# A convolution with a mixture of experts behind it: the copies of a turn ahead of its rests, and one of the weight rests on GpSimd

## The chip, the core and the metric

The kernel runs on one core of one Trainium2 chip. The metric is the device time of one execution in microseconds. What is timed is the whole launch: loads from the chip's memory, all the work, and the stores of the result.

The engines are named as in the profile: PE (TensorE, matrix multiplication), PEld (its weight loads), DVE (VectorE), ACT (ScalarE), POOL (GpSimd), SP (SyncE, which only issues transfers here). Each works off a queue of its own in order. What an engine in front of a wait has behind it in its queue stands still with it.

## The reference

```python
def _attn_ref(x, weight):                 # x (8, 2880, 192), weight (8, 7)
    w = softmax(weight)                   # over the 7 taps of each of 8 heads
    x_pad = np.concatenate([np.zeros((B, 6, D)), x], axis=1)
    ...
    out = np.einsum('hk,bskhg->bshg', w, x_unf)   # causal, 24 channels a head

def _moe_ref(x, w_group, w_expert, w1, w2):       # x (23040, 192)
    g_logits = x @ w_group                        # 4 groups
    g_idx = np.argmax(g_logits, axis=1)
    ...
    for g in range(4):
        e_logits = xg @ w_expert[g]               # 4 experts in a group
        e_idx = np.argmax(e_logits, axis=1)
        ...
            h = np.maximum(xg[mask_e] @ w1[g, e], 0.0)    # 192 -> 1024
            ye = h @ w2[g, e]                             # 1024 -> 192
            out[tok_idx] = (g_w * e_w)[:, None] * ye
```

Each token is first mixed with the six before it, then sent to the best expert of its best group. Only that one of the 16 experts works on it, and the result is weighted by the product of the two softmax values.

## The kernel before

**Two streams of work on one PE.** The router takes the 23040 tokens in 18 units of up to 12 blocks of 120 tokens. Per unit it does the convolution (L452), copies it out of PSUM (L461), stores the mixed rows to memory, computes the 20 logits (L475 to L507), takes softmax and argmax on DVE (L539 to L568), and works out each token's place in the list of its expert (L579 to L626). A matmul of one-hot rows (L633) builds the list, DVE makes it whole numbers (L640, L642), and POOL scatters it into a table in memory (L645) at rows that L626 works out. A unit is a generator, so its pieces are laid between the pieces of the other stream, and the two share every queue.

The other stream is the experts, in slots of 256 tokens. As soon as 5 units are routed, experts 0 to 9 get one slot each (portion 0 of the program, `pi == 0`, from about 115 to 250 us); after 9 units experts 10 to 12 get two, after 12 units experts 13 to 15 three; what is left of each expert's five comes in the last portion, by pairs of slots (`pair`, from about 465 us), and 18 slots of a tail take the remainder.

**A slot.** POOL gathers 256 rows by the list (L717). `turn` transposes them into one PSUM tile `px` and splits them into a high part, a copy rounded to the matmul's format on ACT (L755, `xh`), and a low part, the rest that the rounding left, on DVE (L756, `xl`). The last 64 of the 192 channels go into `xb`, copy and rest in the upper and lower 64 rows: as one copy L766 and one rest L767, or, where the turn is `packed`, as two copies L762 and two rests L763, by turns. A matmul with five products (L817; L786 in a pair) makes the hidden values, ACT and DVE take relu and its rest (L822 and L823; L790 and L791), and two products (L835, L839; L801, L805) lead back to 192 channels. ACT scales them (L897), DVE adds (L898), and POOL scatters the rows into the result (L888).

**Two readers of one tile.** Where ACT and DVE read the same PSUM tile, the framework lets them do so one after the other, in the order in which the program names them. In `turn` all copies and rests read `px`. So a copy that stands behind a rest waits for that rest to end.

**Weights.** `weights()` loads an expert's matrices over SP's queue (L666 to L671) and returns four steps, which `split_one` lays between the matmuls: the first 128 channels of the first matrix into a copy and a rest (`ah` L682 on ACT, `al` L683 on DVE), its last 64 channels (`bh` L690 on ACT, `bl` L691), and the second matrix in two halves (`cw`, L697 on ACT, L698 on DVE). Which engine makes a rest is set by a map, `eng.get(k, nc.vector)`, with 1 for the last 64 channels. For the experts of the portions the map comes from `PENG`, which was empty; experts 0 and 1 are loaded ahead, with a map of their own (empty, before and after); the tail's 18 slots already have POOL make L691. The raw matrices lie in a ring of three buffers (`raw`), so that a load waits for the last rest of the matrix that lay there.

Of the kernel before, what the change touches and what calls it, by code (L numbers as in the profile page):

```python
# [9 lines left out]
F32 = mybir.dt.float32  # L10
# [5 lines left out]
AF = mybir.ActivationFunctionType  # L16
ALU = mybir.AluOpType
# [3 lines left out]
P = 128  # L21
# [3 lines left out]
SLOT = 256  # L25
# [11 lines left out]
def conv_moe_kernel(  # L37
# [10 lines left out]
    nc = tc.nc  # L48
# [26 lines left out]
    D2 = D - P  # L75
# [36 lines left out]
    NTAIL = NBIG + NSMALL  # L112
    LAG = 3
    REST = 10
    PENG = lambda pi, e: None
    NQK = 5
    QREST = 6
    QGA = 0
# [149 lines left out]
    def clear_table():  # L268
# [12 lines left out]
        out=tri, in_=ones, pattern=[[1, P]], compare_op=ALU.is_gt, fill=0.0, base=0, channel_multiplier=-1,  # L281
# [12 lines left out]
    for nb in sorted({n for _, n in units}):  # L294
# [35 lines left out]
        out=sel, in_=ident.rearrange("p (e l) -> p e l", e=E), axis=AX.X, op=ALU.add)  # L330
    nc.gpsimd.iota(io[:, 0:1], pattern=[[0, 1]], base=0, channel_multiplier=1)
    nc.vector.tensor_scalar(
        out=io[:, 1:2], in0=io[:, 0:1], scalar1=LE - 1, scalar2=None, op0=ALU.bitwise_and)
# [6 lines left out]
    for g in range(NSK):  # L340
        nc.sync.dma_start(
            out=skew[0:R, g * HG:(g + 1) * HG],
            in_=bass.AP(wvd.tensor, wvd.offset + VL - KS - (BT - 1) + g * HG * VL, [[1, R], [VL, HG], [1, VW]]),
# [21 lines left out]
    for h in range(H):  # L365
        nc.scalar.activation(
            out=band[0:R, h], in_=skew[0:R, h, BT - 1::-1], func=AF.Exp, bias=wm[0:R, h:h + 1],
# [22 lines left out]
    for i in range(NXG):  # L390
        t = const.tile([P, XE + XW], F32, name=f"xg{i}")
# [347 lines left out]
    def turn(xs, n=2, packed=False, into=None, single=False):  # L739
        if into is None:  # L740
            px = pm.tile([P, 512], F32, name="pm")
            xa = ff.tile([P, 2, SLOT], F32R, name="xa")
            xb = ff.tile([P, SLOT], F32R, name="xb")
            xh, xl = xa[:, 0], xa[:, 1]
        else:
            px = pm.tile([P, 512], F32, name="pm") if single else ph.tile([P, 2, SLOT], F32, name="ph").rearrange("p a b -> p (a b)")
            xh, xl, xb = into
        w = n * P
        for t in range(n):
            nc.tensor.transpose(px[:, t * P:(t + 1) * P], xs[t][:, 1:1 + P], ident)  # L750
            if not packed:
                nc.tensor.transpose(px[0:D2, SLOT + t * P:SLOT + (t + 1) * P], xs[t][:, 1 + P:XW], ident)
        if packed:
            nc.tensor.transpose(px[:, SLOT:SLOT + P], xs[0][:, 1 + P:XE], ident)
        nc.scalar.activation(out=xh[:, 0:w], in_=px[:, 0:w], func=AF.Copy)  # L755
        nc.vector.tensor_tensor(out=xl[:, 0:w], in0=px[:, 0:w], in1=xh[:, 0:w].bitcast(F32), op=ALU.subtract)  # L756
        if packed:
            for t in range(2):
                hi, lo = slice(t * D2, (t + 1) * D2), slice((1 - t) * D2, (2 - t) * D2)
                cs = slice(t * P, (t + 1) * P)  # L760
                pb = px[hi, SLOT:SLOT + P]
                nc.scalar.activation(out=xb[hi, cs], in_=pb, func=AF.Copy)  # L762
                nc.vector.tensor_tensor(out=xb[lo, cs], in0=pb, in1=xb[hi, cs].bitcast(F32), op=ALU.subtract)  # L763
            return None if into else (xa, xb)
        pb = px[0:D2, SLOT:SLOT + w]
        nc.scalar.activation(out=xb[0:D2, 0:w], in_=pb, func=AF.Copy)  # L766
        nc.vector.tensor_tensor(out=xb[D2:P, 0:w], in0=pb, in1=xb[0:D2, 0:w].bitcast(F32), op=ALU.subtract)  # L767
        return xa, xb

    def pair_room():  # L770
        hi = ff.tile([P, 2, SLOT], F32R, name="xa").rearrange("p a b -> p (a b)")
# [4 lines left out]
    def turn_half(X, k, xs, single=False):  # L776
        cs = slice(k * SLOT, (k + 1) * SLOT)
        turn(xs, 2, True, [x[:, cs] for x in X], single)
# [435 lines left out]
    def open_slot(i):  # L1214
# [20 lines left out]
        else:  # L1235
            W = pre.pop(e if pi == 0 else None, None) or weights(e * D, e * F, PENG(pi, e)) if s == 0 else opened[i - 1][0]
            k = [v for v, _ in portions[pi][1]].index(e)
# [12 lines left out]
    while routed[1] < portions[0][0]:  # L1250
# [5 lines left out]
        for i in [i for i, kk in enumerate(KPRE) if kk == k]:  # L1256
            e, q = divmod(i, 5)
# [13 lines left out]
    if TB:  # L1271
        turned[0] = turn(gathered[0])
# [4 lines left out]
    if not TB:  # L1277
        turned[0] = turn(gathered[0])
# [125 lines left out]
    with tc.If(nrare[0] != 0):  # L1404
# [4 lines left out]
        with tc.For_i(0, nover, 1):  # L1409
            for u in range(NU):  # L1410
# [10 lines left out]
                    out=gi[:, 0], in0=gi[:, 1], scalar1=VS.bit_length() - 1, scalar2=None, op0=ALU.logical_shift_right)  # L1421
# [4 lines left out]
                    out=ee, in0=eoff[0:BT].unsqueeze(1).broadcast_to([BT, nb, E]),  # L1426
                    in1=gb[:, 0].unsqueeze(2).broadcast_to([BT, nb, E]), op=ALU.is_equal,
                )
                nc.vector.tensor_tensor(
                    out=ee, in0=ee, in1=ends[0:BT, u].unsqueeze(1).broadcast_to([BT, nb, E]), op=ALU.mult)  # L1430
# [4 lines left out]
                for k in range(nb):  # L1435
                    nc.gpsimd.indirect_dma_start(
                        out=idtab[:, :], out_offset=bass.IndirectOffsetOnAxis(ap=gi[:, 0, k:k + 1].bitcast(U32), axis=0),
                        in_=idw[:, k:k + 1], in_offset=None,
# [50 lines left out]
```

## Time and profile before

| | before |
|---|---|
| median of 3 runs | 1145.64 us (1144.6 to 1146.14) |
| profiled execution | 1152.26 us |
| span of its instructions | 1150.4 us |
| mean granted clock of PE | 0.977 of full speed |
| PE busy | 1072.8 us, 93% |
| DVE busy | 752.4 us, 65% |
| ACT busy | 644.1 us, 56% |
| POOL busy | 523.5 us, 46% |

The span runs from the first to the last instruction of the profiled execution; launch and end are in its time, not in the span. Busy shares are means over a program whose first 115 us (routing alone), the stretch from 115 to 465 us (routing and experts together), the pairs and the tail differ much. A granted clock of 1.0 is 2.4 GHz, one of 0.5 is 1.2 GHz. A row of the timeline gives the start in us from the span's start, the duration in us, engine, line and operation, what is written and read; at its end, in brackets, how long the engine had been idle and whose end it had waited for.

### The profile page before, as it was taken

What the parts mean: (1) busy time and instruction counts of PE and PEld (TensorE: products, weight loads), DVE (VectorE), ACT (ScalarE), POOL (GpSimd) and SP (SyncE); (2) the same over time, 40 slices, a digit from 0 to 9 for tenths busy, and PEclk for the clock granted to TensorE, in tenths of its full rate; (3) what the DMA queues carried; (4) which work ended last, traced back from release to release, by engine and by line L of the source; (5) the groups of instructions that cost most, each with busy time, mean ns of one, the idle gap of its engine ahead of it and who ended that gap; (6) DMA issues with size and microseconds to landing.
All of it is one profiled execution on the core that took longest, in us unless ns stands there. A gap on an engine that the chain in (4) does not pass through costs nothing.

```text
span 1150.4 us, 20931 instructions
## 1 busy us (share of the span) xinstructions
PE 1072.8 (93%) x7124; PEld 971.1 (84%) x7124; DVE 752.4 (65%) x1671; ACT 644.1 (56%) x1362; POOL 523.5 (46%) x611
## 2 busy tenths in 40 slices
PE   6565999998999998999999999999999999999996
PEld 4444788987989998889899999999999988989986
DVE  3465878987778756576565555655556665687874
ACT  5445657765657554454455445554545555677873
POOL 3004143333334454554545454545445554487773
PEclk9878989999999999999999999999999999999998
DMA  8767688999566432332253223322333435499970
GB/s 185 186 158 228 160 222 215 252 234 216 156 155 164 122 106 85 116 112 67 83 137 113 72 76 99 113 74 73 103 101 106 133 92 157 116 257 257 252 201 19
DMA packets 143167, 166.08 MB, mean 144 GB/s; under 512 B 18946, under 2 KB 124397, under 8 KB 143054
## 3 DMA queue, kind: packets, MB, share of 16 engines
q1 hardware_dynamic: 100974, 111.04, 36.4%
q0 software_dynamic: 18752, 35.85, 10.5%
q10 hardware_dynamic: 23328, 17.80, 6.6%
q8 instruction: 57, 0.93, 0.3%
q14 instruction: 56, 0.46, 0.1%
HBM read 129.43 MB, written 36.58 MB: 144 GB/s over the span
## 4 chain that ended last, share of the span: by engine, by line
PE 70%; DMA 5%; DVE 5%; issue 4%; ACT 3%; POOL 1%; POOLq 0%; ACTq 0%; DVEq 0%
PE ph L786 21%; PE ph L817 11%; PE pm L801 7%; PE po L801 7%; PE po L835 7%; PE pm L805 3%; PE po L805 3%; PE po L839 3%; PE pm L452 3%; DMA rawc<-in_moe_w 2%; DMA xg<-xcd,idpt 2%; DVE hl L823 1%; DVE cw L698 1%; PE ph L852 1%; PE ph L750 1%
## 5 line engine op out<-in xcount | busy, mean ns | idle before, releaser
L888 POOL DMA_INDIRECT out<-ys,idp x160 | 174.3, 1090 | 267.9 <-DVE ys L898 192.0
L791 DVE SCALAR_TENSOR_TENSOR hl<-ph,hh 128x512 fp32r<-128x512 f32 x208 | 142.2, 689 | 141.7 <-ACT hh L790 141.3
L790 ACT ACTIVATE hh<-ph 128x512 fp32r<-128x512 f32 x208 | 123.0, 600 | 170.6 <-PE ph L786 167.6
L717 POOL DMA_INDIRECT xg<-xcd,idp x160 | 175.3, 1096 | 93.8 <-issue 40.5
L835 PE MATMUL po<-cw,hh 128*128 128x384 f32 x592 | 193.2, 379 | 3.0 <-DVE ys L898 3.0
L817 PE MATMUL ph<-xa,ah 128*128 128x256 f32 x592 | 169.2, 307 | 0.0
L839 PE MATMUL po<-cw,hl 128*128 128x192 f32 x592 | 149.6, 253 | 0.0
L801 PE MATMUL po<-cw,hh 128*128 128x384 f32 x416 | 134.1, 359 | 0.0
L801 PE MATMUL pm<-cw,hh 128*128 128x384 f32 x416 | 133.9, 359 | 0.0
L823 DVE SCALAR_TENSOR_TENSOR hl<-ph,hh 128x512 fp32r<-128x512 f32 x148 | 101.1, 684 | 42.7 <-ACT hh L822 42.5
L822 ACT ACTIVATE hh<-ph 128x512 fp32r<-128x512 f32 x148 | 87.9, 596 | 62.3 <-PE ph L817 49.8
L835 PEld LDWEIGHTS po<-cw,hh 128*128 128x128 f32 x592 | 112.7, 190 | 7.6 <-DVE ys L898 3.6
L817 PEld LDWEIGHTS ph<-xa,ah 128*128 128x128 f32 x592 | 113.1, 191 | 4.4 <-issue 1.5
L839 PEld LDWEIGHTS po<-cw,hl 128*128 128x128 f32 x592 | 114.4, 193 | 2.0
L805 PE MATMUL pm<-cw,hl 128*128 128x192 f32 x416 | 104.2, 250 | 0.0
L805 PE MATMUL po<-cw,hl 128*128 128x192 f32 x416 | 104.1, 250 | 0.0
L786 PE MATMUL ph<-xa,ah 128*128 128x512 f32 x208 | 86.0, 413 | 1.4 <-DVE hl L791 1.4
L698 DVE TENSOR_TENSOR cw<-rawc,cw 128x768 fp32r<-128x768 f32 x82 | 76.0, 955 | 15.1 <-ACT cw L697 14.5
L817 PE MATMUL ph<-xb,bh 128*128 128x256 f32 x296 | 84.0, 284 | 0.7 <-DVE xb L767 0.7
L805 PEld LDWEIGHTS po<-cw,hl 128*128 128x128 f32 x416 | 79.1, 190 | 5.8
L817 PE MATMUL ph<-xb,bl 128*128 128x256 f32 x296 | 83.9, 284 | 0.0
L817 PE MATMUL ph<-xa,al 128*128 128x256 f32 x296 | 83.7, 283 | 0.0
(275 smaller groups left out, 2656.2 us busy)
## 6 DMA issues: line engine op xcount, KB each, us to landing
rawc<-in_moe_w SPq DMA_DIRECT2D x82, 384.0 KB
raw<-in_moe_w SPq DMA_DIRECT2D x41, 512.0 KB
raw<-in_moe_w SPq DMA_DIRECT2D x82, 256.0 KB
xcd<-xc ACTq DMA_DIRECT2D x13, 1085.6 KB
xin<-in_x SPq DMA_DIRECT2D x7, 1134.0 KB
xc<-in_moe_w SPq DMA_DIRECT2D x18, 384.0 KB
xin<-in_x SPq DMA_DIRECT2D x6, 1039.5 KB
xin<-in_moe_w SPq DMA_DIRECT2D x9, 512.0 KB
```

Of the source, the lines that this page charges most:

```text
L717: nc.gpsimd.indirect_dma_start(out=xs[t][:, 0:XW], out_offset=None, in_=xcd[0:known, :], in_offset=bass.IndirectOffsetOnAxis(ap=ids[:, t, ...
L786: nc.tensor.matmul(out=hp.rearrange("p a b -> p (a b)"), lhsT=W[wgt][:, fs], rhs=xx, start=i == 0, stop=i == len(ops) - 1)
L790: nc.scalar.activation(out=hh, in_=hp, func=AF.Relu)
L791: nc.vector.scalar_tensor_tensor(out=hl, in0=hp, scalar=0.0, in1=hh.bitcast(F32), op0=ALU.max, op1=ALU.subtract,)
L801: nc.tensor.matmul(out=oo[t][:, 0:2 * D], lhsT=hh[:, ts], rhs=cw[:, f].rearrange("p a d -> p (a d)"), start=f == 0, stop=False,)
L805: nc.tensor.matmul(out=oo[t][:, 0:D], lhsT=hl[:, ts], rhs=cw[:, f, 0, :], start=False, stop=f == NF - 1,)
L817: nc.tensor.matmul(out=hp[:, j], lhsT=wgt[:, fs], rhs=xx, start=i == 0, stop=i == len(ops) - 1)
L822: nc.scalar.activation(out=hh, in_=hp, func=AF.Relu)
L823: nc.vector.scalar_tensor_tensor(out=hl, in0=hp, scalar=0.0, in1=hh.bitcast(F32), op0=ALU.max, op1=ALU.subtract,)
L835: nc.tensor.matmul(out=oo[t][:, 0:2 * D], lhsT=hh[:, j, ts], rhs=cw[:, f].rearrange("p a d -> p (a d)"), start=f == 0, stop=False,)
L839: nc.tensor.matmul(out=oo[t][:, 0:D], lhsT=hl[:, j, ts], rhs=cw[:, f, 0, :], start=False, stop=f == NF - 1,)
L888: nc.gpsimd.indirect_dma_start(out=outviews[nscat[0] % len(outviews) if view is None else view], out_offset=bass.IndirectOffsetOnAxis(ap=i ...
```

## The change

Two edits. In `turn`, the copies of the last 64 channels (now L759 where packed, L762 where not) come right behind the copy of the first 128, and the rests (now L763 for the first 128, L767 packed, L771 not) behind all copies. No instruction is added or taken away. And `PENG` now names GpSimd for the rest of the last 64 channels in portion 0, which experts 2 to 9 take from it.

```diff
--- before.py
+++ after.py
@@ -112,7 +112,7 @@
     NTAIL = NBIG + NSMALL
     LAG = 3
     REST = 10
-    PENG = lambda pi, e: None
+    PENG = lambda pi, e: {1: nc.gpsimd} if pi == 0 else None
     NQK = 5
     QREST = 6
     QGA = 0
@@ -753,19 +753,23 @@
         if packed:
             nc.tensor.transpose(px[:, SLOT:SLOT + P], xs[0][:, 1 + P:XE], ident)
         nc.scalar.activation(out=xh[:, 0:w], in_=px[:, 0:w], func=AF.Copy)
+        if packed:
+            for t in range(2):
+                hi, cs = slice(t * D2, (t + 1) * D2), slice(t * P, (t + 1) * P)
+                nc.scalar.activation(out=xb[hi, cs], in_=px[hi, SLOT:SLOT + P], func=AF.Copy)
+        else:
+            pb = px[0:D2, SLOT:SLOT + w]
+            nc.scalar.activation(out=xb[0:D2, 0:w], in_=pb, func=AF.Copy)
         nc.vector.tensor_tensor(out=xl[:, 0:w], in0=px[:, 0:w], in1=xh[:, 0:w].bitcast(F32), op=ALU.subtract)
         if packed:
             for t in range(2):
                 hi, lo = slice(t * D2, (t + 1) * D2), slice((1 - t) * D2, (2 - t) * D2)
                 cs = slice(t * P, (t + 1) * P)
-                pb = px[hi, SLOT:SLOT + P]
-                nc.scalar.activation(out=xb[hi, cs], in_=pb, func=AF.Copy)
-                nc.vector.tensor_tensor(out=xb[lo, cs], in0=pb, in1=xb[hi, cs].bitcast(F32), op=ALU.subtract)
-            return None if into else (xa, xb)
-        pb = px[0:D2, SLOT:SLOT + w]
-        nc.scalar.activation(out=xb[0:D2, 0:w], in_=pb, func=AF.Copy)
-        nc.vector.tensor_tensor(out=xb[D2:P, 0:w], in0=pb, in1=xb[0:D2, 0:w].bitcast(F32), op=ALU.subtract)
-        return xa, xb
+                nc.vector.tensor_tensor(
+                    out=xb[lo, cs], in0=px[hi, SLOT:SLOT + P], in1=xb[hi, cs].bitcast(F32), op=ALU.subtract)
+        else:
+            nc.vector.tensor_tensor(out=xb[D2:P, 0:w], in0=pb, in1=xb[0:D2, 0:w].bitcast(F32), op=ALU.subtract)
+        return None if into else (xa, xb)
 
     def pair_room():
         hi = ff.tile([P, 2, SLOT], F32R, name="xa").rearrange("p a b -> p (a b)")
```

Lines up to 755 keep their numbers; below, L756 becomes L763, L762 becomes L759, L763 becomes L767, L766 becomes L762, L767 becomes L771, and all lines from 772 on move up by four (L817 to L821, L888 to L892).

The queue of POOL at about 114 to 152 us: lists of routed units scattered (L645; the second at 130.6 us, the last of the piece at 151.9 us in the execution before), results scattered (L888), rows gathered (L717). Before:

```order
L645 DMA idtab<-lsi,rowi 377088x1 x2
L888 DMA out<-ys,idp_976 23040x192
L717 DMA xg_211<-xcd,idp_976 128x193
L888 DMA out<-ys,idp_976 23040x192
L717 DMA xg_211<-xcd,idp_976 128x193
L645 DMA idtab<-lsi,rowi 377088x1
```

and with the change:

```order
L645 DMA idtab<-lsi,rowi 377088x1
L691 TENSOR_TENSOR bl<-raw,bh 128x1024
L645 DMA idtab<-lsi,rowi 377088x1
L892 DMA out<-ys,idp_976 23040x192
L717 DMA xg_211<-xcd,idp_976 128x193
L892 DMA out<-ys,idp_976 23040x192
L717 DMA xg_211<-xcd,idp_976 128x193
L691 TENSOR_TENSOR bl<-raw,bh 128x1024
L645 DMA idtab<-lsi,rowi 377088x1
```

The rest for expert 2, 128 rows by 1024, has come in ahead of the second list's scatter, and the one for expert 3 ahead of the third's, behind the same two results and two gathers as before.

The queue of DVE at about 149 us: softmax, running count (`cum`) and, last, the list of one unit (`lsi`), on which the scatter and PE's next convolution wait. Before:

```order
L551 TENSOR_TENSOR ohx<-oh 120x192
L564 TENSOR_TENSOR pick<-ss,oh 120x48
L557 SCALAR_TENSOR_TENSOR cum<-keep_135,ohx 120x192
L565 TENSOR_REDUCE se<-pick 120x12
L691 TENSOR_TENSOR bl<-raw,bh 128x1024
L567 SCALAR_TENSOR_TENSOR se<-se,sg 120x12
L640 TENSOR_SCALAR lv_1752<-pm 128x32
L568 RECIPROCAL xc<-se 120x12
L642 SCALAR_TENSOR_TENSOR lsi<-pm,lv_1752 128x32
```

and with the change:

```order
L551 TENSOR_TENSOR ohx<-oh 120x192
L564 TENSOR_TENSOR pick<-ss,oh 120x48
L557 SCALAR_TENSOR_TENSOR cum<-keep_135,ohx 120x192
L565 TENSOR_REDUCE se<-pick 120x12
L567 SCALAR_TENSOR_TENSOR se<-se,sg 120x12
L568 RECIPROCAL xc<-se 120x12
L640 TENSOR_SCALAR lv_1752<-pm 128x32
L642 SCALAR_TENSOR_TENSOR lsi<-pm,lv_1752 128x32
L827 SCALAR_TENSOR_TENSOR hl<-ph,hh 128x512
L763 TENSOR_TENSOR xa<-pm,xa 128x256
```

The rest for expert 3 has gone from the middle of the chain, and the reciprocal of L568 now comes ahead of L640; behind the chain a rest of a turn (L763) comes right behind L827, as L756 did behind L823.

The queue of ACT at the first pair's two turns, about 457 to 465 us; `xc` in these rows is the room that holds `xb`, `raw` a matrix just loaded. Before:

```order
L897 ACTIVATE ys<-po,xg_217 128x192 x2
L755 ACTIVATE xa<-pm 128x256
L762 ACTIVATE xc<-pm 64x128
L822 ACTIVATE hh<-ph 128x512
L762 ACTIVATE xc<-pm 64x128
L755 ACTIVATE xa<-pm 128x256
L682 ACTIVATE ah<-raw 128x1024
L762 ACTIVATE xc<-pm 64x128
L822 ACTIVATE hh<-ph 128x512
L690 ACTIVATE bh<-raw 128x1024
L762 ACTIVATE xc<-pm 64x128
L790 ACTIVATE hh<-ph 128x512 x2
```

and with the change:

```order
L901 ACTIVATE ys<-po,xg_217 128x192 x2
L755 ACTIVATE xa<-pm 128x256
L759 ACTIVATE xc<-pm 64x128 x2
L826 ACTIVATE hh<-ph 128x512
L755 ACTIVATE xa<-pm 128x256
L759 ACTIVATE xc<-pm 64x128 x2
L682 ACTIVATE ah<-raw 128x1024
L826 ACTIVATE hh<-ph 128x512
L690 ACTIVATE bh<-raw 128x1024
```

Before, the four copies of the last channels (L762) stand each for itself, with a relu (L822) or a weight copy (L682, L690) between them; now each two stand together right behind L755, ahead of both weight copies.

## Rows read from the trace of the kernel before

**Rows 1.** Stretches: length, busy (count) of PE, PEld, DVE, ACT, POOL; PEclk, DMA share, GB/s

```profile
115.00:200.00 85.00, 79.58 (x619) 71.17 (x618) 70.24 (x174) 53.55 (x112) 25.18 (x19) 0.96 0.79 199
560.00:660.00 100.00, 100.00 (x582) 90.56 (x582) 56.47 (x111) 49.02 (x105) 47.71 (x70) 1.00 0.36 96
```

**Rows 2.** Waits of the whole span: engine, tile, line, awaited: us, times, longest

```profile
ACT xc L762 <- DVE lts L756: 38.7, 49, 1.6
ACT xb L766 <- DVE xa L756: 30.3, 30, 3.8
```

**Rows 3.** Waits of PE, whole span, same columns

```profile
PE pm L452 <- DVE lsi L642: 5.3, 2, 2.8
PE ph L786 <- DVE xc L763: 0.9, 1, 0.9
```

**Rows 4.** Instructions of line 691: ns least/median/most, first to last start, forms

```profile
L691 DVE TENSOR_TENSOR bl<-raw,bh x32: 1149/1215/1225, 77.9 to 952.3; 128x1024 fp32r<-128x1024 f32 x32
L691 POOL TENSOR_TENSOR bl<-raw,bh x9: 2389/2407/2413, 991.7 to 1121.8; 128x1024 fp32r<-128x1024 f32 x9
```

**Rows 5.** Timeline, a turn at 126 us: start, us, engine, line, operation, [waited <- releaser]

```profile
125.96 0.38 ACT L766 ACTIVATE xb<-pm 64x256 fp32r<-64x256 f32 x1 [0.68 <-DVE xa L756]
127.25 0.38 PE L817 MATMUL ph<-xb,bh 128*128 128x256 f32 x1 [0.69 <-DVE xb L767]
```

**Rows 6.** Timeline, list scatter at 130 us, first and last of what follows it

```profile
128.94 1.05 ACT L690 ACTIVATE bh<-raw 128x1024 fp32r<-128x1024 f32 x1
130.63 1.00 POOL L645 DMA_INDIRECT idtab<-lsi,rowi  x1 [16.55 <-DVE lsi L642]
138.68 0.16 DVE L626 TENSOR_TENSOR rowi<-rows,goff 128x1 int32<-128x1 f32 x1 [2.56 <-DMA idtab<-lsi,rowi]
140.44 0.45 PE L835 MATMUL po<-cw,hh 128*128 128x384 f32 x1 [1.06 <-DVE ys L898]
```

**Rows 7.** Timeline, VectorE, GpSimd and PE at 146 to 152 us

```profile
146.54 1.79 POOL L717 DMA_INDIRECT xg<-xcd,idp  x1 [0.30 <-issue]
148.94 0.47 DVE L551 TENSOR_TENSOR ohx<-oh 120x192 bf16<-120x192 f32 x1
150.02 1.21 DVE L691 TENSOR_TENSOR bl<-raw,bh 128x1024 fp32r<-128x1024 f32 x1
151.78 1.28 PE L452 MATMUL pm<-xin,band 126*120 126x288 f32 x2 [2.76 <-DVE lsi L642]
```

**Rows 8.** Timeline, tail: a GpSimd rest, a VectorE rest meeting it, one without

```profile
1022.86 2.41 POOL L691 TENSOR_TENSOR bl<-raw,bh 128x1024 fp32r<-128x1024 f32 x1 [1.74 <-ACT bh L690]
1024.17 2.78 DVE L698 TENSOR_TENSOR cw<-xc,cw 128x768 fp32r<-128x768 f32 x2 [0.31 <-ACT cw L697]
1030.32 1.83 DVE L698 TENSOR_TENSOR cw<-rawc,cw 128x768 fp32r<-128x768 f32 x2 [0.31 <-ACT cw L697]
```

**Rows 9.** Timeline, ends of two pauses of PE; busy time of three stretches of 10 us

```profile
254.71 0.54 PE L507 MATMUL pm<-ident,lts 128*120 128x128 f32 x3 [1.56 <-ACT lts L500]
281.81 0.84 ACT L697 ACTIVATE cw<-rawc 128x768 fp32r<-128x768 f32 x1 [2.81 <-DMA rawc<-in_moe_w]
283.56 0.54 PE L507 MATMUL pm<-ident,lts 128*120 128x128 f32 x3 [3.02 <-ACT lts L500]
...
150.00:160.00 10.00, 8.22 (x33) 7.12 (x34) 6.02 (x20) 5.08 (x12) 2.94 (x3) 0.66 0.75 211
250.00:260.00 10.00, 8.44 (x73) 7.06 (x66) 8.61 (x19) 6.36 (x12) 5.27 (x4) 1.00 1.04 285
280.00:290.00 10.00, 6.98 (x35) 5.95 (x34) 6.34 (x18) 4.48 (x10) 4.09 (x4) 0.83 0.72 199
```

**Rows 10.** Timeline, ScalarE and PE at the first pair's turns

```profile
462.85 1.05 ACT L690 ACTIVATE bh<-raw 128x1024 fp32r<-128x1024 f32 x1
463.93 0.27 ACT L762 ACTIVATE xc<-pm 64x128 fp32r<-64x128 f32 x1
464.98 0.50 PE L786 MATMUL ph<-xc,bh 128*128 128x512 f32 x1 [0.93 <-DVE xc L763]
```

## The prediction

> **What bounds the kernel now.** I read busy time by stretch first. From 560 to 660 us, among the pairs, PE is busy for 100.00 of 100 us; from 115 to 200 us, where routing and experts share the queues, for 79.58 of 85 at a mean clock of 0.96, with DVE at 70.24 [rows 1]. So PE sets the end nearly everywhere, and an edit to ACT, DVE or POOL is worth what it takes from a pause of PE. Next come the waits. The copies of the turn look dear: ACT stood for 38.7 us ahead of L762 and 30.3 us ahead of L766 until a rest of DVE had ended, 69 us over 79 waits [rows 2]. PE's own list shows what of it reached PE: one wait of 0.9 us for L763 [rows 3] and one of 0.7 us for L767 [rows 5]. Nothing else in that list names a rest of the turn. All other handoffs lie beside PE's matmuls, since a turn is begun well ahead of the slot that uses it. Where PE is busy all the time they are worth nothing.
>
> Last, the timeline at the places that the change touches. Two matter: the list scattered at 130.6 us, and the list for which PE waited 2.76 us until 151.78 [rows 6, 7] (one of the two waits for `lsi` that sum to 5.3 us [rows 3]). Behind the second lies a cost that no list of waits shows: from 150 to 160 us the granted clock was 0.66 [rows 9]. As the two levels are 1.0 and 0.5, PE ran for 2 x 0.34 x 10 = 6.8 us at 1.2 GHz, which costs up to 3.4 us of work; I take 3.0, since PE was busy for 8.22 of these 10 us.
>
> **The change part by part.** The copies' order adds and removes no instruction, and it lets ACT make both copies back to back.
>
> *The turn at 126 us.* ACT stood 0.68 us for the rest, then made L766 in 0.38; PE stood 0.69 us for what came of it [rows 5]. With the copy ahead of the rest that wait goes: -0.7. But what is late next is the transfer of the list scattered at 130.63: DVE's L626 waited 2.56 us for it until 138.68, and PE's L835 at 140.44 stood 1.06 us behind what DVE does after that [rows 6]. The scatter lands when the other transfers around it let it through, not 8 us after a fixed start, so PE arrives 0.7 earlier and waits 0.7 longer. I put this at 0, with -0.7 as the bound.
>
> *The scatter at 130 us.* The rest for expert 2 now stands ahead of it on POOL. It takes 2.41 us there against 1.215 on DVE [rows 4]. It can start when its copy L690 is done, at 128.94 + 1.05 = 129.99 or, if the turn's 0.7 carries over, at 129.3; it ends at 131.7 to 132.4, and the scatter, at 130.63 before [rows 6], starts 1.1 to 1.8 late. If the landing followed at the same distance, PE's pause at 140 would grow from 1.06 by 1.1 or more; if the landing is set by the other traffic, by nothing. I take +0.5, nearer to the second, because 8 us lie between a scatter of 1.00 us and its landing; bounds 0 and +1.8.
>
> *The list at 149 us.* DVE's rows show no idle time here [rows 7], so taking the rest of 1.21 us out of the chain ahead of `lsi` gives -1.1 (its distance from start to the next start). But POOL, which ended its gather at 146.54 + 1.79 = 148.33, makes it from then to about 150.75. The tail shows what DVE does beside such a rest: POOL's ran from 1022.86 to 1025.27, and two L698 begun in the middle, at 1024.17, took 2.78 us where two alone took 1.83 [rows 8]. The 0.95 us more are about what was left of POOL's rest (1.10). L698 has two inputs in SBUF, as has L551 at 148.94 [rows 7]; begun inside POOL's rest, it would stand until 150.75, 1.8 us, against 1.1 saved: +0.7 for the chain. If it isn't held, -1.1; if it and a later one are, +1.5. I take +0.7, the row nearest in kind, and leave the half-speed stretch behind it as it is.
>
> The Trainium skill says the same from the other side, and against this change: "SBUF — State Buffer", section "Who interferes with whom", has a VectorE instruction with two SBUF inputs and a GpSimd instruction that reads SBUF shut each other out for a whole instruction, the first to issue going first. By that rule the sum stands as it is; without it, it would be 1.8 less at this place. The trace agrees for L698.
>
> *The six other rests*, for experts 4 to 9, from about 165 to 242 us. Each frees 1.2 us of DVE and may hold a two-input operation for up to 2.4 us on POOL. From 200 to 290 us the transfers are the bound: their share is 1.04 from 250 to 260 us [rows 9], and the pause of PE that ends at 283.56 goes back to ACT, whose copy L697 had stood 2.81 us for a transfer of weights until 281.81 [rows 9]; L500, on which PE waited, is behind it on ACT. What DVE gains or loses ahead of such a place is given back there. I put these at 0, with -1 and +2.
>
> *The first pair's turns.* The last copy waited for its turn behind L690, which began at 462.85 and took 1.05, ran at 463.93, and PE stood 0.93 us for its rest until 464.98 [rows 10]. In the new order both copies stand ahead of L690, right behind L755. So -0.9, with work beside it that goes on: no list or transfer is late there.
>
> *Pairs and tail.* PE busy throughout, the tail's rests are on POOL already: 0.
>
> **Sum.** 0 + 0.5 + 0.7 + 0 - 0.9 = +0.3 us on the profiled execution, 1152.26 + 0.3 = 1152.6. That execution is 6.6 us above the median of 1145.64 (three runs from 1144.6 to 1146.14); the same sum on the median gives **1145.9 us**. What a measurement of this kernel can tell from no change is about 0.2%, 2.3 us.
>
> **Rivals.**
>
> *A pause that stays short (faster).* L551 starts ahead of POOL's rest, or isn't held by it. Then the list is ready 1.1 earlier, PE's pause is 1.66 us, about that at 254.7, which was 1.56 and after which the clock stayed at 1.00, where the pauses of 2.76 and 3.02 were each followed by half speed (0.66, and 0.83 from 280 to 290) [rows 7, 9]. The 3.0 us of half speed go too: -1.1 - 3.0 - 0.9 = -5.0, 1140.6 us. For it speaks that L551 stood only 0.6 us behind POOL's earliest start. Against it speaks the held L698. It decides if POOL's rest begins behind L551.
>
> *A pause that grows (slower).* The scatter's start is 1.5 us late and the landing follows. PE's pause at 140.4 goes from 1.06 to about 2.5, near the 2.76 that was followed by half speed; the shorter of such stretches (0.17 x 10 x 2 = 3.4 us, [rows 9]) costs 1.7. With +0.7 at the list and -0.9 at the pair: 1.5 + 1.7 + 0.7 - 0.9 = +3.0, 1148.6 us, and a held operation at one more of the six places would make it 1150. It decides if the transfer lands over 1 us later than 138.6. For it: DVE stood on that landing, with PE behind it. Against: the distance of 8 us is not the scatter's own.
>
> *The edits meet no pause (same).* Scatter and list unchanged, the pair's 0.9 alone, or even that given back: 1144.7 to 1145.6 us. It ends with the forecast on the same side of 2.3 us. For it speaks that 69 us of waits in front of copies left PE only 1.6.
>
> **Chances.** Forecast 0.34, no pause met 0.10, short pause 0.30, grown pause 0.26. The first two are within 0.2%; of their 0.44 I move 0.03 to faster and 0.02 to slower, for half-speed stretches that come or go elsewhere. The likeliest time is the sum's, 1145.9. The range reaches to the rivals on both sides: 1140.0, a little below the faster one's 1140.6, to 1150.0, the slower one's with one more held operation. As the two rivals hold 0.56, the forecast's own range stands beside it: 1144 to 1147.8. Faster by over 0.2% 0.33, same 0.39, slower 0.28.
>
> **What the profile afterwards would show.** ACT's copies without a wait for DVE, and the 69 us of waits moved to DVE ahead of the rest (now L763). PE's waits for `xb` at 127 us and for `xc` at 465 us gone. Eight L691 on POOL of 2.4 us between 129 and 243 us, none on DVE for these experts. L626 waits to about 138.7 (forecast) or 140 (slower). L551 at 149 us with a long duration (forecast) or 0.47 us (faster). The granted clock from 150 to 160 us near 0.66 (forecast) or near 1.0 (faster), and that from 140 to 150 us below 1.0 only in the slower case. The forecast is wrong if PE's pauses outside these places move: if one of the six other rests holds a chain ahead of a list, or if the half-speed stretch behind 283 us comes or goes because the transfers shift.

## The result, and the profile after

The changed kernel took 1152.72 us in the median of 5 runs (1151.4 to 1158.17), the kernel before 1145.86 (5 runs, 1144.6 to 1146.58): a ratio of 1.0077, with a 95% interval of 1.006 to 1.0095. It is slower by 6.9 us in the medians, about 8.8 by the ratio, which is not that of the two medians. That is outside the predicted range, which ended at 1150.0, and on the side of the rival that was given 0.26.

The two profiled executions can't simply be set against each other: their spans are 1150.4 before and 1150.5 after. The first profile of the kernel before was taken from an execution of 1152.26 us, 6.4 above its median. A second one (run `base`, below) is from an execution of 1146.67 us, and later rows of the kernel before are taken from it. Its first slot began at 111.7 us, that of the first profile at 117.9 and the changed kernel's at 113.4, though the edits touch nothing ahead of that slot's turn. So I compare from the first slot's first matmul on. The time from there to the first pair was 344.9 us (before), 342.5 (base) and 350.7 (after); the first matmuls of the slot and of the pair are these, first in base, then in the changed kernel:

```profile
111.73 0.50 PE L817 MATMUL ph<-xa,ah 128*128 128x256 f32 x1
454.23 0.41 PE L786 MATMUL ph<-xa,ah 128*128 128x512 f32 x1
...
113.40 0.50 PE L821 MATMUL ph<-xa,ah 128*128 128x256 f32 x1
464.09 0.41 PE L790 MATMUL ph<-xa,ah 128*128 128x512 f32 x1
```

So 8.2 us against base, 5.8 against the first profile, are lost by the first pair. Part comes back in the pairs and the tail: at the end of the span 4.0 and 4.6 us are left.

Busy time by stretch, the kernel before (base) and the changed kernel; columns as in [rows 1]:

```profile
130.00:140.00 10.00, 8.36 (x56) 7.64 (x49) 7.78 (x18) 4.79 (x9) 4.95 (x3) 0.83 0.32 94
150.00:200.00 50.00, 49.61 (x391) 44.99 (x390) 43.69 (x101) 36.56 (x77) 21.45 (x18) 1.00 0.95 229
```

```profile
130.00:140.00 10.00, 6.64 (x50) 5.45 (x43) 6.12 (x17) 5.34 (x9) 3.06 (x2) 0.88 0.28 78
140.00:150.00 10.00, 8.19 (x52) 7.59 (x50) 9.38 (x19) 1.21 (x3) 6.30 (x5) 0.78 0.59 160
150.00:200.00 50.00, 45.55 (x337) 41.25 (x339) 39.32 (x78) 33.59 (x72) 22.90 (x17) 0.97 0.84 210
```

From 150 to 200 us the changed kernel's PE issues 337 matmuls where it issued 391, and its clock is below 1.00 in each of the three stretches; in base it is 0.83 from 130 to 140 us and 1.00 from there to 200. With levels of 1.0 and 0.5 that is about 9.8 us at half speed against 3.4, so by estimate up to 3.2 us of the lag is clock. DVE looks less busy from 150 to 200 us (39.32 for 43.69), and the transfers' share is lower too: everything waits.

The rests of line 691 in the changed kernel, columns as in [rows 4]:

```profile
L691 DVE TENSOR_TENSOR bl<-raw,bh x24: 1149/1215/1226, 73.9 to 953.8; 128x1024 fp32r<-128x1024 f32 x24
L691 POOL TENSOR_TENSOR bl<-raw,bh x17: 2370/2402/2824, 124.7 to 1121.9; 128x1024 fp32r<-128x1024 f32 x17
```

Eight rests have moved, at 2.40 us each, as costed. What they do to DVE is seen where they run. Two places of the changed kernel's timeline:

```profile
143.91 3.08 DVE L547 TENSOR_TENSOR oh<-sc,mx 120x240 f32<-120x240 f32 x1
144.32 2.39 POOL L691 TENSOR_TENSOR bl<-raw,bh 128x1024 fp32r<-128x1024 f32 x1
149.63 0.72 PE L452 MATMUL pm<-xin,band 126*120 126x288 f32 x2 [1.81 <-DVE lsi L642]
...
159.69 2.56 POOL L691 TENSOR_TENSOR bl<-raw,bh 128x1024 fp32r<-128x1024 f32 x1 [1.88 <-ACT bh L690]
159.92 3.14 DVE L608 TENSOR_TENSOR ohl<-iop,posb 120x768 f16<-120x768 f32 x1
163.25 0.68 DVE L827 SCALAR_TENSOR_TENSOR hl<-ph,hh 128x512 fp32r<-128x512 f32 x1
163.99 0.39 PE L821 MATMUL ph<-xa,ah 128*128 128x256 f32 x1 [2.42 <-DVE hl L827]
```

L547 takes 0.40 us elsewhere in the same trace and 3.08 here; L608 takes 0.95 and, at 159.92, 3.14. Both end about their usual time behind the end of POOL's rest (146.71, 162.25). Neither shows a wait in brackets: the time is in the operation's own duration, so no list of waits names it. PE at 163.99 is charged to `hl` of L827, which was only queued behind the held L608 on DVE; in e10_turn_free (below), where L608 is not held, PE has no wait on `hl` there; its one wait from 148 to 166 us, 1.55 us, is on the next list.

Adding up all DVE operations between 100 and 470 us that took over 0.3 us longer than the shortest of their kind in the same trace gives the time held: 0 in both profiles of the kernel before, and 10.8 us in six operations after (2.68 at 143.91, 2.21 at 159.92, 1.97 at 180.49, 2.21 at 196.92, 0.49 at 216.63, 1.23 at 244.21). All six have two inputs in SBUF. The rests at 124.66 and 227.40 met no such operation.

Of the other predicted signs: the copies of the turn no longer wait for a rest of DVE, and what is left of the handoff stands on DVE, for less than the 69 us of [rows 2]:

```profile
DVE lts L763 <- ACT xc L759: 8.5, 8, 3.2
DVE xa L763 <- ACT xb L762: 5.4, 9, 0.8
```

PE's waits for the last rest of a turn, near 127 us and at the first pair [rows 3, 5], are gone. And the scatter of the list stood behind expert 2's rest, with the pause behind it grown from 1.06 us [rows 6] to 2.45:

```profile
127.20 1.02 POOL L645 DMA_INDIRECT idtab<-lsi,rowi  x1
134.44 0.16 DVE L626 TENSOR_TENSOR rowi<-rows,goff 128x1 int32<-128x1 f32 x1 [3.85 <-DMA idtab<-lsi,rowi]
136.41 0.45 PE L839 MATMUL po<-cw,hh 128*128 128x384 f32 x1 [2.45 <-DVE ys L902]
```

### The profile page after: what moved, and what is told of

Its sections match the earlier page's. It is cut to its first block, busy times and chain, and to the rows that moved or that the text cites. A ratio compares the mean times of both kernels' runs of the same rounds, so it can differ in the third digit from the quotient of the medians.

```text
span 1150.5 us, 20870 instructions
## 1 busy us (share of the span) xinstructions
PE 1076.4 (94%) x7124; PEld 973.5 (85%) x7124; DVE 759.0 (66%) x1663; ACT 639.3 (56%) x1362; POOL 546.7 (48%) x619
## 3 DMA queue, kind: packets, MB, share of 16 engines
q0 software_dynamic: 18752, 35.85, 10.8%
## 4 chain that ended last, share of the span: by engine, by line
PE 74%; DMA 8%; DVE 6%; issue 6%; ACT 3%; POOL 2%; SPq 0%; POOLq 0%; ACTq 0%; DVEq 0%
PE ph L790 20%; PE ph L821 11%; PE pm L805 7%; PE po L839 7%; PE po L805 7%; PE pm L452 3%; PE po L843 3%; PE pm L809 3%; PE po L809 3%; DMA xcd<-xc 2%; DMA idtab<-lsi,rowi 2%; PE ph L856 1%; DMA xg<-xcd,idpt 1%; DMA rawc<-in_moe_w 1%; PE pm L475 1%
## 5 line engine op out<-in xcount | busy, mean ns | idle before, releaser
L892 POOL DMA_INDIRECT out<-ys,idp x160 | 172.1, 1076 | 246.1 <-DVE ys L902 178.8
L717 POOL DMA_INDIRECT xg<-xcd,idp x160 | 174.5, 1091 | 94.5 <-issue 48.4
L821 PE MATMUL ph<-xa,ah 128*128 128x256 f32 x592 | 170.1, 309 | 2.4 <-DVE hl L827 2.4
L827 DVE SCALAR_TENSOR_TENSOR hl<-ph,hh 128x512 fp32r<-128x512 f32 x148 | 100.8, 684 | 44.6 <-ACT hh L826 42.0
L821 PEld LDWEIGHTS ph<-xa,ah 128*128 128x128 f32 x592 | 113.7, 192 | 6.9 <-DVE hl L827 3.2
L698 DVE TENSOR_TENSOR cw<-rawc,cw 128x768 fp32r<-128x768 f32 x82 | 75.8, 955 | 13.6 <-ACT cw L697 11.6
L821 PE MATMUL ph<-xb,bh 128*128 128x256 f32 x296 | 84.2, 284 | 0.0
L821 PE MATMUL ph<-xb,bl 128*128 128x256 f32 x296 | 84.2, 284 | 0.0
L821 PE MATMUL ph<-xa,al 128*128 128x256 f32 x296 | 84.1, 284 | 0.0
```

What stands on the lines that cost most here:

```text
L717: nc.gpsimd.indirect_dma_start(out=xs[t][:, 0:XW], out_offset=None, in_=xcd[0:known, :], in_offset=bass.IndirectOffsetOnAxis(ap=ids[:, t, ...
L821: nc.tensor.matmul(out=hp[:, j], lhsT=wgt[:, fs], rhs=xx, start=i == 0, stop=i == len(ops) - 1)
L827: nc.vector.scalar_tensor_tensor(out=hl, in0=hp, scalar=0.0, in1=hh.bitcast(F32), op0=ALU.max, op1=ALU.subtract,)
L892: nc.gpsimd.indirect_dma_start(out=outviews[nscat[0] % len(outviews) if view is None else view], out_offset=bass.IndirectOffsetOnAxis(ap=i ...
```

## The experiments

Three theories stood at first. P: a rest on POOL holds the DVE operations that have two inputs in SBUF. Q: it delays the list's scatter, or other work, behind it on POOL. T: the new order of the turn costs the time. All ratios are to runs of the kernel before on the same chip, with a 95% interval, from 6 to 12 runs of each changed kernel. The chips differ: the kernel before had a median of 1148.26 us on that of runs e1 to e4, 1149.48 on that of e5 to e7 and base, and 1146.03 on that of e8 to e10, so a median goes with its ratio alone. "Held" is the sum over long DVE operations, as above.

**The turn alone** (run e1_turn): the changed kernel with the empty map.

```diff
-    PENG = lambda pi, e: {1: nc.gpsimd} if pi == 0 else None
+    PENG = lambda pi, e: None
```

> Only the turn's new order; every rest of the weights stays on VectorE. Theory P (GpSimd's rest shuts out VectorE operations with two SBUF inputs) and theory Q (GpSimd's rest makes the list's scatter behind it late) both put the whole loss on the rests: 1145.0 to 1146 us here, as before, or 0.9 us less from the first pair's turn. Theory T (the turn's order loses the time, since the first rest now ends one copy later): about 1152 us.

Measured: 0.9993 (0.997 to 1.0017), median 1145.94; held 0. T is out. The turn's gain can't be told from nothing either, although PE's wait at the first pair is gone. Some may have been given back later: its profile has a new wait of 1.25 us on `ys` and one of 0.58 on `hl` about 10 us behind the first pair's start.

**The rests alone** (run e2_rest): the kernel before with the changed map.

```diff
-    PENG = lambda pi, e: None
+    PENG = lambda pi, e: {1: nc.gpsimd} if pi == 0 else None
```

> Only the rests on GpSimd for experts 2 to 9; the turn in its old order. P and Q: 1151 to 1155 us, as with both edits. T: about 1146 us.

Measured: 1.0074 (1.0046 to 1.0102), median 1155.21; held 10.2 us. The whole loss lies in this edit.

**Expert 2 alone, and experts 3 to 9 alone** (runs e3_rest2, e4_rest3to9), both with the old turn.

```diff
+    PENG = lambda pi, e: {1: nc.gpsimd} if pi == 0 and e == 2 else None
...
+    PENG = lambda pi, e: {1: nc.gpsimd} if pi == 0 and e > 2 else None
```

> The rest of expert 2 alone on GpSimd, old turn. In the changed kernel this rest (124.66 to 127.06 us) held no VectorE operation, but the list's scatter stood behind it. P: 1145.9 us, no change. Q: the scatter starts about 1.5 us late, PE's pause behind it grows by about 1.4 us and is followed by half speed: +1.4 to +4.5, 1147.3 to 1150.4 us.

> The rests of experts 3 to 9 on GpSimd, that of expert 2 on VectorE, old turn. P: VectorE operations held at five or six places for 8 to 11 us together, of which PE sees 2 to 6: 1148 to 1152 us. Q: the scatters behind the rests have little waiting on them: 1145.9 to 1147 us.

Measured: 0.9998 (0.9972 to 1.0024), held 0, and 1.0086 (1.0055 to 1.0117), held 9.1 us. The loss is with the experts whose rests hold something, and it is larger than the 2 to 6 us that I expected PE to see of it: 0.86% is 9.9 us. The first run is weaker against Q than it was meant to be: with the old turn the scatter stayed ahead of the rest in POOL's queue (124.70 and 125.77 us in its trace). Run e9 below makes up for that.

**A rest that reads and writes, and a fill that only writes** (runs e5_read, e6_write). DVE keeps all its rests; behind each, GpSimd does work that nobody needs, on the raw matrix. The map is `{20: None}` in portion 0; the key 20 only marks experts 2 to 9.

```diff
+                if 20 in eng:
+                    nc.gpsimd.tensor_tensor(out=rb, in0=rb, in1=bh.bitcast(F32), op=ALU.subtract)
...
+                if 20 in eng:
+                    for _ in range(2):
+                        nc.gpsimd.memset(rb, 0.0)
```

> The kernel before, in which GpSimd makes a second, unused rest of the last 64 channels for experts 2 to 9, into the raw matrix, after VectorE's own: the same 128x1024 with two inputs read from SBUF, about 2.4 us each, nothing taken from VectorE and no matmul waiting for it. P (VectorE's two-input operations are held for as long as GpSimd reads): held at several places for about 10 us together, 1150 to 1158 us, 0.4 to 0.9% slower than before. Rival R (the time goes because the weights come 1.2 us later out of a slower engine, or because the change puts another order on VectorE's queue): within 0.2% of before. Rival Q (GpSimd's queue, or the raw matrix freed later for its next load): slower here, and as much so in the run that only writes.

> The same place, engine and matrix, but GpSimd only writes: two fills of 128x1024, together about 2.3 us by the 0.52 us of a 128x450 fill. P, in its form that only GpSimd's reads hold VectorE: no operation held, within 0.2% of before. Q: as slow as the run that reads.

Measured: 1.007 (1.0043 to 1.0097), median 1156.78, held 7.6 us; and 0.9988 (0.9965 to 1.0011), median 1147.12, held 0. The two runs use the same engine, the same matrix and the same place, and hold back the same next load. The fills were somewhat shorter, 2 x 0.954 us for 2.374. One pair of rows makes the difference plain. In the reading run:

```profile
210.40 2.37 POOL L693 TENSOR_TENSOR raw<-raw,bh 128x1024 f32<-128x1024 f32 x1 [4.88 <-DVE off L583]
210.91 0.17 DVE L585 TENSOR_TENSOR ends<-pm,ends 128x16 f32<-128x16 f32 x1
210.99 2.00 DVE L588 TENSOR_TENSOR pos<-cum,off 120x192 f32<-120x192 bf16 x1
```

and in the writing run:

```profile
210.12 1.97 POOL L694 MEMSET raw<- 128x1024 f32 x2 [4.83 <-DVE bl L691]
210.66 0.17 DVE L585 TENSOR_TENSOR ends<-pm,ends 128x16 f32<-128x16 f32 x1
210.74 0.35 DVE L588 TENSOR_TENSOR pos<-cum,off 120x192 f32<-120x192 bf16 x1
```

L588 reads `cum` and `off`, both in SBUF: 2.00 us beside a reading GpSimd, to 0.2 us behind its end, and 0.35 beside a writing one. L585 has one input in PSUM (`pm`) and takes 0.17 beside either. So R (a later `bl`, another order on DVE) and Q are out as causes of the loss, and P stands.

**The same without the hold** (run e7_free, old turn; run e10_turn_free, new turn). For experts 2 to 9 the rest is left out: the low part of their last 64 channels' weights is zero.

```diff
+                if 20 in eng:
+                    nc.gpsimd.tensor_copy(out=bl[:, 0:1], in_=bh[:, 0:1])
+                    for _ in range(2):
+                        nc.gpsimd.memset(bl.bitcast(F32), 0.0)
+                else:
                     eng.get(k, nc.vector).tensor_tensor(out=bl, in0=rb, in1=bh.bitcast(F32), op=ALU.subtract)
```

> The kernel before, in which the rest of the last 64 channels is left out for experts 2 to 9: GpSimd copies one column and fills the tile with zeros twice, as long as its rest would take. VectorE is freed of eight rests (9.7 us), GpSimd is as busy as in the change, nothing of 2.4 us is read. P: what the change was worth without the hold: the pause before the convolution at 151.8 us shorter by 1.1 us, and with it perhaps its half-speed stretch: 0 to 5 us faster, 1141 to 1146 us. R or Q: as slow as the change, 1152 us or more.

> The changed kernel with both edits, but the rest of the last 64 channels is left out for experts 2 to 9: GpSimd copies one column and fills the tile with zeros twice, as in the run with the old turn. It shows what the change as a whole would be worth without the hold. P: no operation held, 0 to 0.4% faster than before. If the two edits hurt one another in another way: slower than before by 0.3% or more.

Measured: 0.9988 (0.9966 to 1.0009), held 0.8 us, and 0.9995 (0.9974 to 1.0015), held 0.35. With DVE freed of eight rests, 9.7 us, and nothing held in exchange, the edit gains at most a few tenths of a per cent. There was next to nothing to win, with or without the new turn.

What is still held here is another kind: an operation with one SBUF input, L566, which begins beside a fill and ends just behind it (the fills end at 177.08, L566 at 177.11). In e10 L566 takes 0.51 us at 173.44 in the same way, and L565 behind it is queued. From e7:

```profile
175.12 1.96 POOL L694 MEMSET bl<- 128x1024 f32 x2
176.47 0.64 DVE L566 TENSOR_SCALAR sg<-ss 120x12 f32<-120x12 f32 x1
```

Its shortest time there is 0.16 us. So a fill is not free for every DVE operation; none of the two-input ones was held by one.

**Four experts each** (runs e8_rest3to6, e9_rest2and7to9), with the new turn.

```diff
+    PENG = lambda pi, e: {1: nc.gpsimd} if pi == 0 and 3 <= e <= 6 else None
...
+    PENG = lambda pi, e: {1: nc.gpsimd} if pi == 0 and not 3 <= e <= 6 else None
```

> The changed kernel, with GpSimd making the rests of experts 3 to 6 alone. In the changed kernel these four held VectorE for 9.1 of the 10.8 us. P, by the time held: nearly the whole loss, 0.5 to 0.9% slower than before, 1152 to 1158 us. If the loss goes by the number of rests: half of it, about +3.5 us.

> The changed kernel, with GpSimd making the rests of experts 2, 7, 8 and 9 alone, which held VectorE for 1.7 of the 10.8 us there. P, by the time held: within 0.2% of before. If the loss goes by the number of rests: half of it, about +3.5 us.

Measured: 1.0045 (1.0023 to 1.0066), held 7.4 us; and 0.9988 (0.9966 to 1.0009), held 1.7. The second run decides: its interval leaves out the +0.3% of a loss by number. The first doesn't, since its size lies between the two forecasts, just under what I expected, and its interval holds both. The two sets of four also run at different places (experts 3 to 6 from 141 to 194 us in e8), so time held and place are not told apart by them; that the hold is the cause is shown by e5 against e6, at the same places. In the second run the scatter again stands behind expert 2's rest, and the pause behind it is as long as in the changed kernel:

```profile
126.13 1.01 POOL L645 DMA_INDIRECT idtab<-lsi,rowi  x1 [0.16 <-issue]
133.16 0.16 DVE L626 TENSOR_TENSOR rowi<-rows,goff 128x1 int32<-128x1 f32 x1 [3.77 <-DMA idtab<-lsi,rowi]
135.13 0.44 PE L839 MATMUL po<-cw,hh 128*128 128x384 f32 x1 [2.38 <-DVE ys L902]
```

Yet this kernel is not slower than the one before. What the late scatter costs at 135 us is not seen in the time.

**The kernel before again** (run base), for its profile.

> The kernel before once more, for a second profile of it. All theories: no operation of VectorE held; PE's pause before the convolution at about 146 to 152 us near 2.8 us, a half-speed stretch behind it; the first slots 3 to 8 us earlier or later than in the first profile, since the stages ahead of them differ from run to run.

Measured: 1146.67 us, held 0. PE's pause before the convolution was not the expected 2.8 us:

```profile
145.32 0.72 PE L452 MATMUL pm<-xin,band 126*120 126x288 f32 x2 [1.25 <-DVE lsi L642]
...
140.00:150.00 10.00, 8.75 (x64) 7.64 (x63) 8.19 (x25) 4.75 (x13) 3.67 (x3) 1.00 0.81 225
150.00:160.00 10.00, 10.00 (x87) 9.65 (x86) 9.93 (x22) 7.80 (x16) 5.19 (x4) 1.00 0.96 230
```

The pause was 1.25 us and no half speed followed it; the half speed had come ahead of it, from 130 to 140 us. But the 2.76 us of [rows 7] and the half speed behind them [rows 9] are no freak of that one execution either. In e3_rest2, of 1146.5 us and with nothing held:

```profile
145.10 0.47 PE L452 MATMUL pm<-xin,band 126*120 126x288 f32 x1 [2.75 <-DVE lsi L642]
...
135.00:145.00 10.00, 6.85 (x54) 6.39 (x54) 9.95 (x25) 1.67 (x3) 5.73 (x4) 1.00 0.63 170
145.00:155.00 10.00, 9.90 (x53) 8.76 (x54) 6.84 (x17) 7.33 (x17) 5.09 (x4) 0.83 0.74 213
```

Both patterns occur, and the length of the pause tells little of the time: counted from the first slot, this convolution began at 33.9 us (before, pause 2.76), 33.6 (base, 1.25) and 33.2 (e3_rest2, 2.75).

## Why the prediction was wrong

**The step that failed is that of the six other rests, put at 0 with bounds of -1 and +2.** The mechanism was named and its row was right: the held L698 of the tail [rows 8]. But it was costed at one place, the list at 149 us, and the other places were written off because the transfers bound the stretch from 200 to 290 us. Measured, the rests of experts 4 to 9 held DVE for 8.1 of the 10.8 us, 6.4 of them in the three between 159 and 197 us, before the stretch for which that reason was given. From 150 to 200 us PE was busy for 49.61 of 50 us in base: a delay that reached PE there had no idle time to go into. One of these three holds can be followed straight to PE, in the 2.42 us at 163.99 shown above. Counted from the first slot and turn by turn, the changed kernel was 2.4 us behind base at the turn at 150.5 us (its own time), 6.4 at 167.9, 8.3 at 187.2, 9.5 at 216.3 and 9.7 at 245.1. Behind the list at 149 us, then, some 7 us were lost by 245 us against base, and some 5 against the first profile (2.1 behind at 150.5, 7.4 at 245.1), where the bound was +2. Part of that is the clock.

The transfers do give something back, but less than I took. Counted in the same way, the changed kernel was 9.3 us behind base at the turn that begins at 255.8 us in base (153.4 against 144.1), 7.3 behind at the one at 286.6 (182.2 against 174.9), and 8.2 at the first pair (350.7 against 342.5).

**The list at 149 us** (+0.7). The mechanism is right, the operation was another. POOL's rest met L547, three operations ahead of L551, and held it for 2.68 us, not 1.8: +1.6 with the 1.1 saved, just past the upper bound of +1.5. With the scatter's term it comes out in the convolution behind it, which began 36.2 us behind the first slot's first matmul, 2.3 to 2.6 later than in the two profiles of the kernel before. What I had seen as the start of the rest, the end of the gather, was right: 144.32 lies 0.03 behind the end of the gather begun at 142.50 (1.79 us long).

**The scatter at 130 us** (+0.5). DVE's wait for the landing grew by 1.3 us (2.56 to 3.85) and PE's pause by 1.4, which looks like the rival's case. Counted from the first slot it isn't. The scatter began 1.0 us later than in either profile before (13.8 for 12.8), but the landing, by the start of L626, came only 0.2 to 0.6 later (21.0 for 20.8 and 20.5), and PE went on 0.4 to 0.8 later (23.0 for 22.6 and 22.3). The pause grew further because PE also came to it earlier: in e1_turn, with the scatter on time, the new turn alone makes it 1.47. So +0.5 was about right, and e9_rest2and7to9, where the scatter began 2.0 later and the landing came 1.0 to 1.4 later, shows no cost in the time.

**The turns.** The 0.7 at 126 us was rightly put at 0: PE came earlier to the pause behind it and waited longer. The -0.9 at the first pair is real as a wait that went away, but e1_turn doesn't show it in the time: its interval holds -0.9 us and 0 alike.

**The rivals.** The slower one had the right sign and named holds at "one more of the six places" as its reserve; that reserve was the main cost, and its first part, the scatter, was not. Its sign in the clock was there too: 0.78 from 140 to 150 us. The faster one fell by its own condition: POOL's rest began at 144.32, ahead of L551 (147.58), and held L547. Its premise was weak too, and this is a second failing, of reading: I took a pause and its clock from a single execution, and priced them as time to be saved, where base and e3_rest2 show that a short and a long pause end at nearly the same time.

The Trainium skill's rule ("SBUF — State Buffer", section "Who interferes with whom") was weighed at one place and not walked along all eight rests, six of which held something. For DVE operations with two SBUF inputs it agrees with the rows here: GpSimd work that reads SBUF holds them (2.00 us for L588 in e5_read), work that only writes does not (0.35 in e6_write).

What stays open: which of the six holds cost PE how much, and how much of it by way of the clock. The holds shift each other, PE's waits behind them are charged to operations that were only queued, and the two profiles of the kernel before differ by up to 3.1 us at the same turn. The 4.0 to 4.6 us left at the end of the profiled spans are also less than the 6.9 of the medians. Why the first 113 us differ by some 6 us from run to run was not looked into.

## What to carry to other kernels

Before work with SBUF inputs goes to GpSimd, list for each place where it will run what stands in VectorE's queue at that time, and add a hold of about the GpSimd operation's length for the first two-input operation that meets it (2.68 us at most here, beside a rest of 2.39); one free place (experts 2 and 8) says nothing of the next. Such a hold is found in a profile by durations, not by waits: compare an operation's time with the shortest of its kind. And before a pause or a clock is costed, take a second profile, and ask when the engine goes on rather than how long it stood.

## What the hardware showed that I had not expected

The hold does not depend on the size of the held operation: a rest of POOL turned an operation on 128x3 elements (L1064, two SBUF inputs) from 0.15 us into 1.97 in e5_read. The recorded start doesn't tell who is held: in the changed kernel L547 began at 143.91, 0.41 us ahead of the rest that held it. It acts the other way too: at 196.43 us in the changed kernel POOL's rest began inside a two-input operation of DVE (L608, 196.05 to 197.00) and took 2.82 us for 2.40. And GpSimd's fill of 128x1024 took 0.954 us in e6_write, 16 times over, without holding anything by over 0.3 us, while in e7_free and e10_turn_free such a fill held the one-input L566.
